# Value loads over the border of two key spans in a banded attention kernel with two expert layers

## The chip, the core and the metric

The kernel runs on one core of a Trainium2 chip. The metric is the device time of one execution in microseconds. The core has a matmul engine (TensorE, PE in the profile, with its weight loads as PEld), a vector engine (VectorE, DVE), a scalar engine (ScalarE, ACT), a general engine (GpSimd, POOL) and a sync engine (SyncE, SP), which issues nearly all loads. Each engine works its own instructions in order. Transfers run on 16 DMA engines.

## The reference

Three layers follow each other on 2 x 768 tokens of width 512. The change concerns the first, an attention in chunks of 32 queries that look at 16 keys to the left, the chunk, 8 keys to the right, and 8 memory keys:

```python
for c in range(nc):                       # chunk = 32
    c_start = c * chunk; c_end = c_start + chunk
    l_start = max(0, c_start - left_ctx)  # 16
    r_end = min(S, c_end + right_ctx)     # 8
    k_full = np.concatenate([mem_k, k[:, :, l_start:r_end]], axis=2)
    v_full = np.concatenate([mem_v, v[:, :, l_start:r_end]], axis=2)
    scores = scale * np.matmul(q[:, :, c_start:c_end], k_full.transpose(0, 1, 3, 2))
    a = np.exp(scores - np.max(scores, axis=-1, keepdims=True))
    a = a / (np.sum(a, axis=-1, keepdims=True) + 1e-09)
    out[:, :, c_start:c_end] = np.matmul(a, v_full)
```

Then comes a gated layer (`h = gelu(x @ w_in)`, halves u and v, v normalised and mixed over the tokens by `w_sg`, `x + (u * v_s) @ w_out`), and then a layer of 8 experts, in which each token takes one expert: `p[e] * (relu(x @ w1[e]) @ w2[e])`.

## The kernel before

The tokens stand in tiles of 128, 6 for each of the 2 batches (`b`, `tt`). For attention, a tile's 8 heads are two groups of four (`h4`, or `g` where loads are named), and its 128 queries two spans of 64 (`u`), each of two chunks (`c`). The host lays values out as `vw[b, tt, g, w, h, u, d]`: for each group 96 rows `w` (8 memory rows, 16 of left context, 64 own, 8 of right context), a row being 4 heads x 2 spans x 65 numbers, the 65th a one that sums the weights. Chunk 0 uses rows 0 to 63 of a span, chunk 1 rows 32 to 95 with the first 8 of them replaced by the memory rows.

The steps of a tile are `Score.load` (queries and two key tiles), `window` (POOL copies the keys of chunk 1 to `kx`), `mm` (scores, L397), `Attn.soft` (maximum on DVE, L416, exponentials on ACT, L420), `turn` (transposes, L428), and for each group of heads `Head.load` (values, L447) and `Head.s0` (32 matmuls at L463, then division by the sum at L472 to L477). `Head.load` fills one tile `v` of 128 rows for one group: partitions 0 to 63 with rows 0 to 63 and partitions 64 to 127 with rows 32 to 95, in one transfer whose source pattern has three levels:

```python
bass.AP(src.tensor, src.offset, [[32 * 8 * DV, 2], [8 * DV, 64], [1, 8 * DV]])
nc.gpsimd.tensor_copy(v[64 : 64 + NM], v[:NM])                        # L451
nc.gpsimd.tensor_scalar_mul(one, one, edge[64 * c : 64 * c + 64])     # L455
```

The copy at L451 puts the memory rows in place for chunk 1. In the first and the last tile of a batch, L455 sets the ones of rows outside the sequence to zero with the mask `edge`. Both stand on POOL directly behind the issue of the load.

`Turn` transposes the result. The classes `Conv64`, `ConvOut` and `conv_sg` turn the weights of the second layer into pairs of a high and a low part (DVE and ACT), `V`, `U`, `Gate` and `X1` are its matmuls, `route1` to `tile_experts` find the experts, and `Moe` runs the expert tiles. All loads of 128 x 512 numbers and all tiles of that size share one ring of 94 slots (`slot`); a load waits on SP for its slot.

What sets the order is the table `ORDER`: each name in it is one step of one item, issued on its engines when the table comes to it (`lv030` is the value load of batch 0, tile 3, group 0, `p030` its head's steps, `lo2` a load of output weights, `pre0` to `pre3` four early loads of the first expert's weights each, which hang on a mark that DVE writes at L1346). The engines' queues have exactly this order. `Moe.run` follows the table.

Of the kernel before, what the change touches and what calls it, by code (L numbers as in the profile page):

```python
# [12 lines left out]
F32 = mybir.dt.float32  # L13
# [6 lines left out]
ALU = mybir.AluOpType  # L20
# [33 lines left out]
a040 p021 p021 a110 lv020 p021 lq00 p020 p020 p031 k000 k001 p020 p020 p031 a041 a111 a111 p021 p031 a041 lv030
s00 p030 a11 a040 a040 a000 lv2 lv050 cv2.0 a01 cv2.0 a001 a04 t011 p030 p030 lv041 cv2.1 a001 p030 t010 a001
a000 a000 cv2.1 cv2.1 cv2.1 cv2.1 cv2.1 t010 p050 a00 a04 p041 a11 t010 cv2.2 cv2.3 lv010 p010 p010 lv040 p040
lq12 k121 t011 t011 v03.0 v03.0 p040 k120 s12 lq14 p010 p010 a121 lv100 ls3 p050 v02.0 p041 p041 p041 a120 p040
p040 v03.1 a00 lv001 a120 p001 lv051 lv000 a120 p050 p050 p051 p051 p051 p051 lq13 ls5 k130 a121 a121 t020 t020
p001 p001 p001 t020 p100 v02.0 p000 k131 v02.1 t021 t021 t021 v02.1 v02.1 s13 a131 a131 a131 p000 v04.0 v04.0
p000 lu1 cu1.0 k140 k141 p100 p100 p100 p000 s14 a140 a141 a130 a12 t000 a12 t000 v04.1 v05.0 v02.1 cu1.0 lv121  # L60
v03.1 v03.1 lv101 a140 t000 v02.1 v02.1 p101 p101 p101 lv110 p101 a140 p121 p121 p121 p110 cu1.1 lq15 k150 lv011
a130 a130 a13 a141 a141 a13 p121 lv111 p011 p011 p011 k151 s15 lo3 p011 v04.1 p111 v04.1 p111 lv130 a150 a151
p110 p110 t001 a14 t001 t001 v00.0 a150 lo0 p111 p111 p110 t100 lu2 a151 cu2.0 lu3 p130 cu2.0 consts2 a151 rx
lv131 p131 p130 p131 p131 p130 ls6 v02.1 v02.2 v05.0 v05.1 a150 a14 a15 a15 t100 t100 v05.1 v05.1 lv140 p140
v01.0 p130 p131 lv151 lx01.0 lx01.1 lv141 ls4 p141 p141 p141 p141 lv150 lu0 cu0.0 cu0.0 p150 p150 p150 cu2.1
cu2.1 lv120 p120 p120 cu2.1 t101 t101 cu2.1 p151 p120 v01.0 t101 v10.0 co0.0 p150 p140 p140 ls8 t111 t111 p120
p140 t110 t110 p151 v01.1 p151 lx00.0 p151 t121 t110 t111 cu0.1 cs3.0 cu3.0 ls0 cu3.0 cu0.1 t120 t120 cu1.1 t121
t120 v01.1 lo1 cu0.1 cu0.1 v12.0 cs8.0 v12.0 v10.0 cu0.1 cu0.1 cu0.2 cu2.1 v10.1 v10.1 cu2.1 lx00.1 lx10.0 cu1.1
lx10.1 cu1.1 cu1.1 cu2.2 v13.0 v11.0 v13.0 t121 v12.1 lx12.0 cu3.1 v01.1 cu3.1 cu3.1 cs0.0 cu3.1 ls7 cu3.1 cu3.1
v10.1 v03.1 cu1.1 cu1.2 cu0.3 v03.1 v03.1 v03.1 co0.0 cu1.3 cu3.2 v15.0 v15.0 lx11.0 v12.1 cu3.3 cu2.3 v12.1  # L70
v12.1 v11.0 v11.1 u10.0 lx11.1 v11.1 v11.1 u10.0 u10.0 v03.2 v12.1 u03.0 u03.0 u11.0 u11.0 ls2 v10.1 v10.1 v10.1
co3.0 v10.1 v14.0 v00.0 v00.1 v00.1 u10.1 v00.1 v00.1 u03.0 cs7.0 v12.1 v10.2 lx12.1 v10.2 v10.2 cs4.0 v14.0
v04.1 v04.1 v15.1 v05.1 v15.1 cs7.1 v03.2 v03.2 v14.1 u15.0 v15.1 cs5.0 u15.0 v04.1 v04.1 ls1 cs1.0 u11.0 u11.1
u01.0 v04.2 v05.1 v05.1 cs4.1 u15.0 v12.1 v12.2 v05.1 u10.1 u11.1 v00.1 v00.1 v00.1 v04.2 u10.1 v13.1 v13.1 u14.0
v00.2 u15.1 u11.1 v13.1 u01.0 v11.1 v00.2 v11.1 u14.0 u02.0 cs2.0 cs2.1 v12.2 co0.1 co0.1 u15.1 cs8.1 u01.0 u01.1
# [41 lines left out]
def tile_kernel(  # L117
# [241 lines left out]
    class Score:  # L359
# [74 lines left out]

    class Head:
# [1223 lines left out]
```

## Time and profile before

| what | value |
|---|---|
| median of 3 runs | 551.38 us (551.11 to 551.87) |
| profiled execution | 553.8 us, span 552.0 us |
| PE busy | 423.3 us (77%) |
| DVE busy | 315.7 us (57%) |
| ACT busy | 179.9 us (33%) |
| POOL busy | 77.6 us (14%) |
| bytes moved | 76.12 MB, mean 138 GB/s |

The span is the profiled execution without what lies around the program. Busy times are sums over stages that differ: the attention and the first of the weight conversions take up the first 180 us, the second layer runs to about 361 us, and the expert tiles from there to the end. The page's chain of what ended last covers only the last scatter and says nothing of the stages before; they are read from the stretches, the waits and the timelines.

### The profile page before, as it was taken

To read this page: it belongs to the slowest core of one execution; us is meant where nothing else is said; L and a number is where in the kernel's file an instruction comes from. 1 tells how busy PE (TensorE), PEld (TensorE's weight loads), DVE (VectorE), ACT (ScalarE), POOL (GpSimd) and SP (SyncE) were. 2 spreads that over 40 slices of the span, in tenths; PEclk is the share of its full clock that TensorE was granted. 3 is DMA by queue.
4 is the path that set the end of the run, shared out by engine and by line. 5 is a ranking of instruction groups with operands and counts; after the bars stand their busy time and mean duration, and the time that the engine had idled before them with its cause. 6 is when DMAs were issued, how large, how long until landed. Compare 5 with 4: busy or idle time off the path is not lost. (4 is left out here: it accounts for less than half of the span.)

```text
span 552.0 us, 10751 instructions
## 1 busy us (share of the span) xinstructions
PE 423.3 (77%) x4055; PEld 363.9 (66%) x4055; DVE 315.7 (57%) x787; ACT 179.9 (33%) x405; POOL 77.6 (14%) x154
## 2 busy tenths in 40 slices
PE   1735363836252999981998899979999999999993
PEld 0524242625141889981998797867989889696882
DVE  5725021513311799992598688948996774725450
ACT  1823020501200455430123201015765643625330
POOL 3411011211211001010000000003200302110101
PEclk9865585855675899996899899989999999999998
DMA  8631424224323000003002001379999798991000
GB/s 272 201 124 51 132 67 140 88 87 152 97 98 115 23 20 20 2 1 114 1 1 78 0 1 59 114 250 385 386 318 374 229 379 284 349 384 50 34 3 33
DMA packets 43389, 76.12 MB, mean 138 GB/s; under 512 B 5581, under 2 KB 12625, under 8 KB 43330
## 3 DMA queue, kind: packets, MB, share of 16 engines
q1 hardware_dynamic: 39362, 65.46, 35.1%
q0 software_dynamic: 2240, 6.75, 3.3%
q10 hardware_dynamic: 1728, 3.15, 1.5%
q8 instruction: 34, 0.56, 0.4%
q14 instruction: 25, 0.20, 0.1%
HBM read 69.04 MB, written 6.75 MB: 137 GB/s over the span
## 5 line engine op out<-in xcount | busy, mean ns | idle before, releaser
L463 PE MATMUL xp<-v,at 64*32 64x65 f32 x768 | 32.4, 304 | 76.3 <-DMA v<-in_vw 58.3
L188 DVE TENSOR_TENSOR we_l<-raw,we_h 128x512 fp32r<-128x512 f32 x128 | 81.3, 688 | 3.1 <-ACT we_h L183 2.3
L463 PEld LDWEIGHTS xp<-v,at 64*32 64x32 f32 x768 | 22.9, 157 | 86.7 <-issue 35.3
L183 ACT ACTIVATE we_h<-raw 128x512 fp32r<-128x512 f32 x105 | 58.7, 629 | 1.1 <-PE wot L280 1.1
L645 PE MATMUL vsp<-sg_h,vh_h 128*128 128x256 f32 x144 | 43.1, 299 | 17.0 <-DVE gtmp L658 17.0
L472 DVE TENSOR_SCALAR rs<-xp 128x4 f32<-128x4 f32 x24 | 3.6, 158 | 91.3 <-PE xp L463 91.2
L1217 PE MATMUL hp<-xe_h,we_h 128*128 128x256 f32 x160 | 45.4, 284 | 0.0
L1217 PE MATMUL hp<-xe_l,we_h 128*128 128x256 f32 x160 | 45.0, 282 | 0.0
L1217 PE MATMUL hp<-xe_h,we_l 128*128 128x256 f32 x160 | 44.9, 281 | 0.0
L645 PE MATMUL vsp<-sg_l,vh_h 128*128 128x256 f32 x144 | 42.1, 293 | 0.0
L645 PE MATMUL vsp<-sg_h,vh_l 128*128 128x256 f32 x144 | 42.0, 292 | 0.0
L1293 PE MATMUL op<-we_h,ht_h 128*128 128x512 f32 x104 | 41.8, 402 | 0.1
L1293 PE MATMUL op<-we_h,ht_l 128*128 128x512 f32 x104 | 41.1, 395 | 0.5 <-DVE ht_l L188 0.5
L1293 PE MATMUL op<-we_l,ht_h 128*128 128x512 f32 x104 | 41.1, 395 | 0.2 <-DVE we_l L188 0.2
L645 PEld LDWEIGHTS vsp<-sg_h,vh_h 128*128 128x128 f32 x144 | 29.0, 201 | 17.7 <-DVE gtmp L658 17.7
L451 POOL COPY v<-v 8x520 f32<-8x520 f32 x24 | 14.8, 616 | 127.0 <-DMA v<-in_vw 114.6
L1305 POOL DMA_INDIRECT out_dram<-o,sidx x15 | 15.8, 1054 | 119.7 <-ACT o L1304 90.8
L1217 PEld LDWEIGHTS hp<-xe_h,we_h 128*128 128x128 f32 x160 | 30.2, 189 | 0.1
L1217 PEld LDWEIGHTS hp<-xe_l,we_h 128*128 128x128 f32 x160 | 30.1, 188 | 0.0
L1217 PEld LDWEIGHTS hp<-xe_h,we_l 128*128 128x128 f32 x160 | 30.2, 189 | 0.0
L1249 DVE SCALAR_TENSOR_TENSOR ht_l<-hp,ht_h 128x512 fp32r<-128x512 f32 x20 | 13.7, 688 | 28.1 <-ACT ht_h L1248 28.1
L645 PEld LDWEIGHTS vsp<-sg_l,vh_h 128*128 128x128 f32 x144 | 29.1, 202 | 0.0
(286 smaller groups left out, 1060.4 us busy)
## 6 DMA issues: line engine op xcount, KB each, us to landing
raw<-in_w SPq DMA_DIRECT2D x160, 256.0 KB
v<-in_vw SPq DMA_DIRECT2D x24, 260.0 KB
k<-in_kw SPq DMA_DIRECT2D x24, 192.0 KB
raw_in<-in_w_in SPq DMA_DIRECT2D x16, 256.0 KB
q<-in_qT SPq DMA_DIRECT2D x12, 256.0 KB
x1d<-x ACTq DMA_DIRECT2D x12, 256.0 KB
rsg<-in_w_sgT SPq DMA_DIRECT2D x9, 256.0 KB
raw_out<-in_w_out SPq DMA_DIRECT2D x8, 256.0 KB
```

The source lines that it names most:

```text
L183: nc.scalar.activation(hi, src, AF.Copy)
L188: nc.vector.tensor_tensor(lo, src, hi.bitcast(F32), ALU.subtract)
L451: nc.gpsimd.tensor_copy(v[64 : 64 + NM], v[:NM])
L463: nc.tensor.matmul(xp[64 * u + 32 * c : 64 * u + 32 * c + 32, j, :], at[64 * c : 64 * c + 64, 2 * u + self.h4, 32 * j : 32 * j + 32], v[64 ...
L472: nc.vector.tensor_scalar_add(rs, xp[:, :, D], 1e-9)
L645: nc.tensor.matmul(self.ps[:, h * 256 : (h + 1) * 256], self.vh[s].hl[wa][:, f * 128 : (f + 1) * 128], rhs_sg(wb, s, self.g), start=(s == ...
L1217: nc.tensor.matmul(ps[:, i * 256 : (i + 1) * 256], self.w[f // 4 * 4 + k][wa][:, f % 4 * 128 : (f % 4 + 1) * 128], self.x[k // 2][wb][:, k ...
L1249: nc.vector.scalar_tensor_tensor(l, self.ps[s], 0.0, h.bitcast(F32), ALU.max, ALU.subtract)
L1293: nc.tensor.matmul(self.po[c], h[wa][:, o : o + 128], self.w[8 + k][wb], start=(k == 0 and n == 0), stop=(k == 7 and n == 2),)
L1305: nc.gpsimd.indirect_dma_start(dst, bass.IndirectOffsetOnAxis(ap=sidx[:, c : c + 1], axis=0), o, None, bounds_check=NT * 512 // n - 1, oob ...
```

## The change

A value tile no longer belongs to one group of heads. The rows of all 24 spans of keys (2 batches x 6 tiles x 2 groups, 96 rows each) are seen as one list, and load `n` takes 128 rows in a row from row 32 of span `n`: partitions 0 to 63 get rows 32 to 95 of span `n` (its chunk 1), partitions 64 to 127 rows 0 to 63 of span `n + 1` (the next one's chunk 0). There are 25 loads, `n` from -1 to 23, the first and the last of 64 rows. A head reads two tiles: chunk 0 from `vt[n - 1]`, chunk 1 from `vt[n]`. The memory rows are copied from tile `n - 1` to tile `n` in a step of its own (`mem_v`, named `m...` in the table); the masking stays with the load. The halves of the scores, of their transposes and of `edge` are swapped to match. The table `ORDER` is a new one.

```diff
 ORDER = """
-lv1 cv1.0 cv1.0 cv1.1 cv1.1 consts1 lv0 cv0.0 edges lq02 cv0.0 cv0.1 cv0.1 cv0.1 cv0.1 cv0.1 cv0.1 k021 k020 lq03
+lv0 consts1 cv0.0 edges cv0.0 lv2 cv0.1 cv0.1 cv0.1 cv0.1 cv2.0 lq01 k011 cv2.0 cv2.1 cv2.1 cv2.1 cv2.1 cv2.1
...
-                                self.sc[u][32 * j : 32 * j + 32, 2 * g + c, :],
+                                self.sc[u][32 * j : 32 * j + 32, 2 * g + 1 - c, :],
...
+    vt = {}
+
+    def load_v(n):
+        t = vt[n] = slot([128, 4, 2, DV], F32, f"v{n}")
+        p0, p1 = 64 if n < 0 else 0, 64 if n == NB - 1 else 128
+        r0 = n * W + 32
+        nc.sync.dma_start(
+            t[p0:p1].rearrange("p h u d -> p (h u d)"),
+            vw.rearrange("b t g w h u d -> (b t g w) (h u d)")[r0 + p0 : r0 + p1],
+        )
+        for p, u, m, e in ((0, 1, n, TT - 1), (64, 0, n + 1, 0)):
+            if 0 <= m < NB and m // 2 % TT == e:
+                one = t[p : p + 64, :, u, D]
+                nc.gpsimd.tensor_scalar_mul(one, one, edge[p : p + 64])
+
+    def mem_v(n):
+        nc.gpsimd.tensor_copy(vt[n][:NM], vt[n - 1][64 : 64 + NM])
...
-        def load(self):
-            b, tt, g = self.b, self.tt, self.h4
-            v = self.v = slot([128, 4, 2, DV], F32, f"v{self.n}")
-            src = vw[b, tt, g].rearrange("w h u d -> w (h u d)")
-            nc.sync.dma_start(
-                v.rearrange("p h u d -> p (h u d)"),
-                bass.AP(src.tensor, src.offset, [[32 * 8 * DV, 2], [8 * DV, 64], [1, 8 * DV]]),
-            )
-            nc.gpsimd.tensor_copy(v[64 : 64 + NM], v[:NM])
...
+                        ks = slice(64 - 64 * c, 128 - 64 * c)
                         nc.tensor.matmul(
                             xp[64 * u + 32 * c : 64 * u + 32 * c + 32, j, :],
-                            at[64 * c : 64 * c + 64, 2 * u + self.h4, 32 * j : 32 * j + 32],
-                            v[64 * c : 64 * c + 64, j, u, :], start=True, stop=True,
+                            at[ks, 2 * u + self.h4, 32 * j : 32 * j + 32],
+                            vt[n - 1 + c][ks, j, u, :], start=True, stop=True,
```

SP's queue where the value loads begin, before (`raw_in` are weights of the second layer, `q` and `k` queries and keys):

```order
L447 DMA v_573<-in_vw 128x1x520
L447 DMA v_659<-in_vw 128x1x520
L369 DMA q_663<-in_qT 128x2x256
L373 DMA k_665<-in_kw 128x384
L373 DMA k_667<-in_kw 128x384
L447 DMA v_710<-in_vw 128x1x520
L200 DMA raw_in_0_777<-in_w_in 128x512
L200 DMA raw_in_1_779<-in_w_in 128x512
L447 DMA v_781<-in_vw 128x1x520
L447 DMA v_806<-in_vw 128x1x520
```

The same place now:

```order
L445 DMA v_491<-in_vw 128x520
L445 DMA v_559<-in_vw 128x520
L445 DMA v_564<-in_vw 128x520
L445 DMA v_593<-in_vw 128x520
L371 DMA q_654<-in_qT 128x2x256
L375 DMA k_656<-in_kw 128x384
L375 DMA k_658<-in_kw 128x384
L445 DMA v_705<-in_vw 128x520
L445 DMA v-1_717<-in_vw 64x520
L445 DMA v_737<-in_vw 128x520
```

The source is 128 x 520 instead of 128 x 1 x 520, one load has 64 rows, and the loads stand in the order of the spans, so that neighbours come together.

POOL's queue at the same place, before (L177, L386: key copies; L451: memory rows; L455: mask):

```order
L451 COPY v_573<-v_573 8x520
L451 COPY v_659<-v_659 8x520
L177 COPY kx_690<-k_665 128x4x56
L177 COPY kx_690<-k_665 128x4x8
L386 COPY k_665<-k_665 64x4x16
L177 COPY kx_690<-k_667 128x4x56
L177 COPY kx_690<-k_667 128x4x8
L386 COPY k_667<-k_667 64x4x16
L451 COPY v_710<-v_710 8x520
L451 COPY v_781<-v_781 8x520
L455 TENSOR_SCALAR v_781<-v_781,edge 64x4
```

POOL's queue now (L179, L388: key copies; L455: memory rows, from the tile before; L452: mask):

```order
L455 COPY v_564<-v_559 8x520
L455 COPY v_559<-v_491 8x520
L455 COPY v_491<-v_593 8x520
L179 COPY kx_660<-k_656 128x4x56
L179 COPY kx_660<-k_656 128x4x8
L388 COPY k_656<-k_656 64x4x16
L179 COPY kx_660<-k_658 128x4x56
L179 COPY kx_660<-k_658 128x4x8
L388 COPY k_658<-k_658 64x4x16
L455 COPY v_705<-v_564 8x520
L452 TENSOR_SCALAR v-1_717<-v-1_717,edge 64x4
L452 TENSOR_SCALAR v_737<-v_737,edge 64x4
```

Each copy of memory rows names two tiles, and key copies stand between the load's mask and the next copy.

SP's queue at the last loads of the second layer's weights, before (`rsg` the mixing weights, `raw_out` the output weights, `raw` expert weights, `x1d` a row of zeros, TENSOR_LOAD an expert's number read into a register):

```order
L310 DMA rsg_2208<-in_w_sgT 128x512
L310 DMA rsg_2311<-in_w_sgT 128x512
L1126 DMA raw<-in_w 128x512 x4
L200 DMA raw_out_0_2729<-in_w_out 128x512
L200 DMA raw_out_1_2731<-in_w_out 128x512
L1126 DMA raw<-in_w 128x512 x4
L1075 DMA x1d<-zero 1x512
L1110 TENSOR_LOAD eid_97
```

The same place now:

```order
L315 DMA rsg_2189<-in_w_sgT 128x2x256
L202 DMA raw_out_0_2349<-in_w_out 128x512
L202 DMA raw_out_1_2351<-in_w_out 128x512
L315 DMA rsg_2360<-in_w_sgT 128x2x256
L312 DMA rsg_2476<-in_w_sgT 128x512
L1134 DMA raw<-in_w 128x512 x16
L1083 DMA x1d<-zero 1x512
L1118 TENSOR_LOAD eid_97
L1118 ISA x2
L1580 TENSOR_LOAD eids
```

The last output weights have moved ahead of all sixteen early expert loads, which stand in one run, and the finished table of expert numbers (`eids`) is read directly behind the first number (`eid`).

## Rows read from the trace of the kernel before

**Rows 1.** The page's 40 slices of 13.8 us: TensorE clock, transfer share, GB/s.

```profile
PEclk9865585855675899996899899989999999999998
DMA  8631424224323000003002001379999798991000
GB/s 272 201 124 51 132 67 140 88 87 152 97 98 115 23 20 20 2 1 114 1 1 78 0 1 59 114 250 385 386 318 374 229 379 284 349 384 50 34 3 33
```

**Rows 2.** Stretches: us, busy (instructions) of PE, PEld, DVE, ACT, POOL; clock, DMA share, GB/s.

```profile
0.00:180.00 180.00, 82.03 (x1657) 62.00 (x1660) 56.62 (x192) 41.03 (x136) 36.92 (x111) 0.68 0.39 125
180.00:361.00 181.00, 163.95 (x1219) 150.94 (x1209) 145.75 (x387) 52.24 (x105) 8.42 (x13) 0.94 0.10 34
361.00:552.00 191.00, 177.33 (x1192) 150.92 (x1190) 113.32 (x209) 86.64 (x164) 32.27 (x30) 0.98 0.71 248
```

**Rows 3.** Waits up to 180 us: engine, line, waited for; us, times, longest.

```profile
POOL v L451 <- DMA v<-in_vw: 114.6, 22, 8.1
...
PE xp L463 <- DMA v<-in_vw: 58.3, 15, 9.3
...
PE xp L463 <- POOL v L455: 13.1, 4, 6.5
```

**Rows 4.** Timeline of POOL, 145 to 180 us: start, us, operation [idle before].

```profile
148.04 0.61 POOL L451 COPY v<-v 8x520 f32<-8x520 f32 x1 [8.11 <-DMA v<-in_vw]
...
165.44 0.61 POOL L451 COPY v<-v 8x520 f32<-8x520 f32 x1 [4.73 <-DMA v<-in_vw]
...
178.61 0.61 POOL L451 COPY v<-v 8x520 f32<-8x520 f32 x1 [6.18 <-DMA v<-in_vw]
```

**Rows 5.** Shorter stretches, columns as in rows 2.

```profile
10.00:15.00 5.00, 2.61 (x155) 2.13 (x160) 4.03 (x11) 0.80 (x2) 4.82 (x14) 1.00 1.04 371
14.00:28.00 14.00, 9.90 (x411) 7.67 (x393) 10.52 (x33) 11.12 (x45) 6.05 (x22) 0.88 0.61 195
48.00:54.00 6.00, 4.62 (x41) 3.83 (x32) 4.53 (x12) 4.24 (x14) 0.63 (x2) 0.50 0.13 49
98.00:112.00 14.00, 10.61 (x188) 8.11 (x179) 7.41 (x22) 7.36 (x24) 2.79 (x10) 0.87 0.28 92
148.00:154.00 6.00, 2.49 (x36) 1.67 (x36) 3.39 (x9) 1.60 (x3) 1.19 (x2) 0.50 0.13 49
400.00:420.00 20.00, 20.00 (x105) 16.82 (x104) 15.50 (x27) 11.54 (x23) 0.91 (x1) 1.00 0.99 328
```

**Rows 6.** The page's DMA issues: count and KB of each.

```profile
v<-in_vw SPq DMA_DIRECT2D x24, 260.0 KB
```

**Rows 7.** Timeline, first 12 us: first load, its first reader, first matmul.

```profile
0.83 1.82 SPq L200 DMA_DIRECT2D raw_in<-in_w_in  x4
...
3.95 0.29 DVE L220 TENSOR_SCALAR cv_in<-raw_in 128x256 uint32<-128x256 uint32 x1 [3.95 <-DMA raw_in<-in_w_in]
...
11.16 0.47 PE L397 MATMUL sc<-k,q 64*32 64x64 f32 x16 [11.16 <-DMA k<-in_kw]
```

**Rows 8.** Timelines of SP, DVE and PE, 244 to 260 us.

```profile
248.76 1.75 SPq L1126 DMA_DIRECT2D raw<-in_w  x4
250.61 0.86 SPq L200 DMA_DIRECT2D raw_out<-in_w_out  x2
...
255.53 0.29 DVE L220 TENSOR_SCALAR cv_out<-raw_out 128x256 uint32<-128x256 uint32 x1 [6.84 <-DMA raw_out<-in_w_out]
...
259.56 0.58 PE L645 MATMUL vsp<-sg_h,vh_h 128*128 128x256 f32 x1 [12.75 <-DVE gtmp L658]
```

**Rows 9.** A dense stretch, columns as in rows 2.

```profile
200.00:220.00 20.00, 20.00 (x152) 19.14 (x151) 18.20 (x41) 12.78 (x25) 3.44 (x5) 1.00 0.10 27
```

**Rows 10.** Waits of SP's queue up to 180 us, columns as in rows 3.

```profile
SPq L313 <- PE xp L463: 10.4, 1, 10.4
...
SPq L369 <- POOL v L455: 4.3, 1, 4.3
```

More of the change, by code (lines that the diff above doesn't have):

```diff
@@ L29 @@
 NU = 12
+NB = 24
 UQ = 64
@@ L54 @@
[L54 to L63, printed above, removed]
@@ new lines @@
+cv1.1 k010 s01 a011 a010 a010 a011 a021 a021 cv1.1 cv1.1 cv1.1 cv1.1 k031 s03 lq05 k051 a011 cv3.0 cv1.2 a02 a031
+a031 cv0.3 a031 a010 cv3.0 cv3.1 cv3.1 k050 cv3.1 a02 lq11 k110 s05 a050 a050 k111 lq00 k001 a01 a01 k000 a030
+s11 a111 a030 a030 a111 lv020 a051 a051 a051 cv3.1 cv3.1 cv3.1 a050 a110 a110 a03 a03 s00 a000 a000 a000 lv021
+cv3.2 lv030 m030 a05 p030 a001 lv011 cv1.3 m021 p021 p030 p030 p021 p030 m020 p020 p020 p020 p020 a001 a001 a00
+a00 lq10 k100 k101 s10 a101 lv031 a110 a05 t010 m031 lv p031 lv000 p021 p021 a111 m000 a11 p031 p031 p031 p000
@@ new lines @@
+m111 p111 lu2 cu2.0 cu1.1 p120 a14 t111 v01.1 p130 p130 t110 v03.1 lu3 t110 lx01.0 lx01.1 v03.2 v03.2 p111 p111
+p111 v01.1 cs0.0 p101 p101 p101 v00.1 lo0 p140 p140 t100 p151 cu2.0 lx02.0 t111 t110 v12.0 v02.1 v00.1 cu0.0
+v02.1 v02.1 p140 lx02.1 cu2.1 cu2.1 p151 p151 p151 t101 m150 p150 t100 cu2.1 t100 cu3.0 cu3.0 t101 cu2.1 cu2.1
+v00.1 p150 p141 t101 v10.0 v02.2 p150 p150 v11.0 p140 lx11.0 p141 v04.0 cu0.1 cu2.1 cu0.1 cu0.1 p141 p141 v00.1
+v00.1 t121 v04.1 v04.1 v04.1 ls4 t120 t120 t121 v00.1 t121 t120 cu3.1 lx00.0 cu3.1 cu3.1 cu0.1 cu0.1 ls2 cu3.1
@@ new lines @@
+lg11.0 lg02.0 pre1 pre2 pre3 g14.1 g14.1 x02.1 g11.1 lg02.1 lg01.0 lg01.1 lg00.0 lg00.1 x10m0 r0 r0 r0 x12m1
+x12m2 x12m3 x12.1 x12.2 lg11.1 x02.2 x10m1 r1 x01h0 lg10.0 r1 r1 r1 r1 r1 r1 lg10.1 x10m2 x10m3 g15.1 r2 cm4
+lg12.0 lg12.1 cm5 x13m0 x13m1 R1 x10.1 R1 R1 x03h0 x05.1 r2 x01h1 x01.1 r4 x01.2 r2 r5 x13m2 r5 R2 r5 R2 R2 R2 R2
+r5 R2 x03h1 x03.1 r5 r6 r6 r6 r6 x04h0 R3 zero R3 x10.2 R2 x03.2 g15.1 r6 r6 x13m3 x13.1 x13.2 R3 RM RP r6 RP RP
+RA RA RA r5 RA RA x00h0 x00h1 x00.1 x00.2 RA RA RP RA RA x04h1 RP RP RP r5 r5 r7 x05.2 RP x04.1 r5 x11m0 x11m1
@@ L98 @@
+x11m2 x04.2 x11m3 x14m0 x11.1 x14m1 x11.2 x14m2 x14m3 x15m0 x15m1 RP RP x15m2 RA RA RP RP RP RP RP x15m3 RP RP RP
+RP R2 RP RP RP x14.1 RP RP RP RP RP RS RZ x15.1 RL XL RZ G0 cm6 cm7 r1 R4 r3 RE RT RE XL RO x15.2 RT RS x14.2 G2
+G1 RT RT RP RT XL RA XL
 """.split()
@@ L440, in __init__ @@
             self.n = f"{b}{tt}{h4}"
-        def load(self):
-            b, tt, g = self.b, self.tt, self.h4
-            v = self.v = slot([128, 4, 2, DV], F32, f"v{self.n}")
-            src = vw[b, tt, g].rearrange("w h u d -> w (h u d)")
-            nc.sync.dma_start(
-                v.rearrange("p h u d -> p (h u d)"),
-                bass.AP(src.tensor, src.offset, [[32 * 8 * DV, 2], [8 * DV, 64], [1, 8 * DV]]),
-            )
-            nc.gpsimd.tensor_copy(v[64 : 64 + NM], v[:NM])
-            for t, c in ((0, 0), (TT - 1, 1)):
-                if tt == t:
-                    one = v[64 * c : 64 * c + 64, :, c, D]
-                    nc.gpsimd.tensor_scalar_mul(one, one, edge[64 * c : 64 * c + 64])
         def s0(self):
             xp = bank([128, 4, DV], "xp")
-            at, v = attns[self.b][self.tt].at, self.v
+            at, n = attns[self.b][self.tt].at, (self.b * TT + self.tt) * 2 + self.h4
             for j in range(4):
@@ L1485, in tile_kernel @@
     at("edges", edges)
+    at("lv", load_v, -1)
     at("consts1", consts1)
@@ L1502, in tile_kernel @@
                 at(f"a{b}{i}{u}", attns[b][i].soft, u)
-                at(f"lv{b}{i}{u}", heads[b][i][u].load)
+                at(f"lv{b}{i}{u}", load_v, (b * TT + i) * 2 + u)
+                at(f"m{b}{i}{u}", mem_v, (b * TT + i) * 2 + u)
                 at(f"p{b}{i}{u}", heads[b][i][u].s0)
```

75 lines of the change are left out of this document (34 added, 41 removed).

## The prediction

> **What bounds the kernel now.** I read the page's 40 slices first. The transfer engines, which reach a busy share of 0.9 and 385 GB/s in the expert part, stand at 0.1 to 0.4 and 51 to 152 GB/s in the ten slices from 41 to 180 us, and TensorE's granted clock moves between 0.5 and 0.8 there [rows 1]. The stretches by stage say the same in sums: in the first 180 us PE is busy 82.03 us at a mean clock of 0.68, DVE 56.62, ACT 41.03, POOL 36.92, and 125 GB/s come in; from 180 to 361 us PE is busy 163.95 of 181, so that part is dense [rows 2]. No engine is the bound of the first part. The waits name what is: POOL waited 114.6 us for the value loads ahead of its copy at L451, PE 58.3 us for them directly and 13.1 us for POOL's scaling behind them [rows 3].
>
> The pace of that wait shows in POOL's timeline: from 148.04 to 178.61 us each copy comes 6.1 us after the one before (six copies, five gaps), and the last five waited 4.7 to 6.2 us for a load [rows 4]. In stretches in which only value loads are under way (48 to 54 and 148 to 154 us) 49 GB/s move at a busy share of 0.13, about 2 of 16 engines [rows 5]. That is not slow memory: per busy engine it is 49/(0.13 x 16) = 23.6 GB/s, and in the stretch from 10 to 15 us, with query, key and weight loads, 371/(1.04 x 16) = 22.3 GB/s [rows 5]. So a value load uses two engines at full rate and fourteen not at all. A load is 260 KB, 266,240 bytes [rows 6]: 266.2/49 = 5.4 us at that rate. All of SP's loads go through the same two engines, so whatever is queued behind a value load shares its pace.
>
> **The change part by part.**
>
> The loads. The source of a value load was a pattern of 2 x 64 x 520 (two overlapping windows of a span), now it is 128 x 520 without the two; the shape in the order is that of the query and weight loads, 128 rows. I take it that the load then spreads over all engines as those do: 266.2/371 = 0.72 us instead of 5.4. The bytes stay: 23 loads of 260 KB and two halves, 6,240 KB, are the 24 of before. The transfer time that leaves engines 0 and 1 is 24 x (5.4 - 0.72) = 112 us; that is the ceiling of the gain, and what is next late takes a part of it back.
>
> The Trainium skill, "DMA: Bandwidth & Descriptors", section "Why a DMA increments its semaphore by 16 and not by 1", has the count of engines as the largest number up to 16 that divides the slowest dimension of both patterns, so 2 before and 16 after. The trace agrees on the first half, by its share of 0.13 [rows 5]; no run here shows the second half yet. By that rule the sum below stands as it is; without it the third rival's 538.7 would be as near.
>
> What is next late in the first 180 us. The work there stays, so each resource's own length bounds the stage:
> - DMA: 180 us x 125 GB/s = 22.5 MB; at 371 GB/s 61 us, plus 3.1 us from the first issue to the first landing [rows 7]: 64 us.
> - ACT: 41.03 us. In its fullest stretch, 14 to 28 us, ACT is busy 11.12 of 14 (0.794) [rows 5]: 51.7 us, plus 11 us before its work begins: 63 us.
> - DVE: 56.62 at 10.52/14 = 0.751 [rows 5] is 75.4 us, plus 3.95 us until its first load lands [rows 7]: 79 us.
> - PE: 82.03 us at clock 0.68. Two attention stretches in which PE, DVE and ACT all have work have a clock of 0.88 and 0.87 and PE shares of 9.90/14 = 0.707 and 10.61/14 = 0.758 [rows 5]. Scaled by the clock, 82.03 x 0.68/0.88 = 63.4 and 82.03 x 0.68/0.87 = 64.1; divided by the shares 89.6 and 84.6; plus 11.16 us until the first matmul [rows 7]: 101 and 96 us.
> PE is the longest, so I take 97, near the denser of its two readings since the loads no longer hold either. The stage goes from 180 to 97: **83 us off**. The ends are 79 us (DVE's length, PE no obstacle) and 127 us (clock stays as it is on average: 82.03/0.707 + 11.16).
>
> The two tiles of a head. Each head's 32 matmuls now read two tiles, the halves swapped; number and form are those of before, so nothing on PE. The copy of the memory rows (24 on POOL, of 8 x 520) takes its source from the neighbouring tile: number and size stay. It is now a step of its own and no longer sits directly behind its load, so POOL's key copies don't queue behind a landing; only the eight scalings still do. What is added is that a head waits for two landings: 0 if loads run ahead, 24 x 0.72 = 17 us if each head finds the second one missing. SP issues runs of three or four value loads ahead of their copies, so I take 0 and leave 17 to the range.
>
> The order's other move. At 248.76 us SP sent four expert weight loads (they hang on DVE's mark) and only behind them the two parts of an output weight; DVE, in order, sat at that weight's conversion until 255.53, and PE 12.75 us for DVE's gate product, to 259.56 [rows 8]. The new order has all output weights ahead of all sixteen early expert loads, in one run. Nothing else was late there (both engines idle), so I take the whole **12.75 us off**; if the gap only moves, 0.
>
> From 361 us on (191.0 us [rows 2]) the sixteen loads come earlier, but SP now reads the finished table of expert numbers before its first load by number, where it had sixteen such loads ahead of that before; I set the two against each other at nothing, with 4 us either way.
>
> **Sum.** The profiled execution took 553.8 us: 553.8 - 83 - 12.75 = 458.0. The median of the runs is 2.4 us below that execution, so 455.6.
>
> **The rivals.**
> 1. Dense first stage: PE follows DVE's length, 79 instead of 97 us: 455.6 - 18 = 437.6. For it: the two engines' lengths are near each other, and 200 to 220 us shows an order that keeps both over 0.9 [rows 9]. Against: attention is a chain over POOL, PE, DVE, ACT and back for every tile, and neither of its two full stretches had PE over 0.76 [rows 5].
> 2. The clock stays low: many short matmuls with gaps leave PE at 1.2 GHz as from 48 to 54 us (0.50) [rows 5]. The stage is 127 us, the time 455.6 + 30 = 486. For it: half of that stage's slices ran so [rows 1]. Against: the gaps there are the waits for values, and 98 to 112 us had 0.87. The Trainium skill, "TensorE: Matmul & The Clock Gate", "What's actually happening", says that the throttled state is the default and activity lifts it; the trace agrees in sign, 0.50 beside 1.00 in the dense stretch from 400 us [rows 5].
> 3. The loads stay on two engines, because what confines them is the length of a row (520 numbers, as before) and not the pattern's two windows: then only the 12.75 us go: 553.8 - 12.75 - 2.4 = 538.7. Against: the weight loads' rows of 512 numbers are about as long and are among those that ran at a share of 1.04 [rows 5].
> 4. Slower: slots. All tiles come from one ring of 94 slots, a value tile now lives until two heads have read it, and SP issues in order. The first 46 loads and what is computed from them use up the ring, so the 52 loads from there to the expert weights can each have to wait for a slot. Such a wait was 4.3 us or 10.4 us where it showed [rows 10]. If all 52 paid 4.3 us unhidden, that is 224 us: 455.6 + 224 = 680. It turns the gain of 96 us into a loss from 96/52 = 1.8 us a load on. Against: the life of a slot is counted in work, and the work of the stage is done sooner.
>
> **How the numbers follow.** Forecast 62% (443 to 470), dense stage 16%, low clock 15%, two engines 3%, slots 2%; 2% that it lands within 0.2%, about what a measurement of this kernel can tell from no change. The range reaches to the first rival with the 4 us of the last part, 437.6 - 4 = 433.6, and to the second, 486, which holds the 17 us of the second tile too; what lies beyond (a third of the first two rivals, the last two and the 2%) is 17%. Faster: 62 + 16 + 15 + 3 = 96%.
>
> **What would show it.** Value loads land at over 300 GB/s, and the transfer share in the first 60 us is above 0.6; the wait of POOL and PE for values falls below 20 us in sum. The last value copy, at 178.61 us before, comes at 85 to 105 us. The gap of 12.75 us is gone. The part from the first load by expert number to the end is 187 to 195 us. Wrong if value loads keep a share of 0.13; if the attention ends before 85 or after 115 us; or if PE has a new gap of over 10 us between the attention and the routing.

## The result and the profile after

The changed kernel takes 441.75 us (median of 4 runs, 439.59 to 442.58) against 551.25 us (551.11 to 551.87): a ratio of 0.801, with an interval of 0.798 to 0.804. The profiled execution took 441.88 us, its span is 440.1 us. That is 13.9 us less than predicted, inside the range of 433.6 to 486 us and on the side that was forecast, but 1.3 us below the 443 to 470 us that had the largest chance.

The page's 40 slices of the changed kernel, 11 us each (they answer to [rows 1]; the first line is PE's busy share in tenths):

```profile
PE   0677879999999998899999689999999999999991
PEclk9898999999999999999999959999999999999996
DMA  7999890102200011000813369999789889910001
GB/s 265 364 320 364 278 315 15 49 26 73 72 25 1 1 52 45 1 1 1 300 59 130 110 214 397 331 387 363 248 269 375 283 279 396 379 41 24 19 5 40
```

The transfers that crept along for 180 us are now done in the first six slices, 66 us, at 265 to 364 GB/s a slice. The granted clock, 0.5 to 0.8 there before, is at 0.8 or more up to a single dip in front of the expert tiles.

To compare the stages I cut both kernels at two events: the end of the last matmul of the attention, and the first matmul of an expert tile (L1240 before, L1248 after). The stretches of before, cut in this way (columns as in [rows 2]: length, busy us and count of PE, PEld, DVE, ACT and POOL, granted clock, transfer share, GB/s):

```profile
0.00:182.40 182.40, 84.44 (x1697) 63.72 (x1697) 57.83 (x197) 41.94 (x138) 36.92 (x111) 0.67 0.38 123
182.40:371.80 189.40, 168.91 (x1228) 155.52 (x1225) 148.67 (x402) 51.95 (x106) 9.67 (x14) 0.94 0.14 48
371.80:552.00 180.20, 169.97 (x1134) 144.61 (x1134) 109.19 (x190) 86.03 (x163) 31.02 (x29) 0.99 0.70 248
```

And those of the changed kernel:

```profile
0.00:87.80 87.80, 63.30 (x1725) 49.65 (x1725) 63.74 (x212) 48.11 (x150) 39.45 (x113) 0.96 0.74 247
87.80:258.00 170.20, 161.13 (x1197) 147.51 (x1197) 143.53 (x388) 46.70 (x94) 10.83 (x15) 0.98 0.18 62
258.00:440.00 182.00, 171.70 (x1134) 145.95 (x1134) 109.27 (x188) 85.95 (x163) 27.83 (x27) 0.97 0.69 241
```

| part | before, us | after, us | change | of it PE's idle time | of it PE's busy time |
|---|---|---|---|---|---|
| attention | 182.4 | 87.8 | -94.6 | -73.5 | -21.1 |
| second layer and routing | 189.4 | 170.2 | -19.2 | -11.4 | -7.8 |
| expert tiles | 180.2 | 182.0 | +1.8 | +0.1 | +1.7 |

(Idle is length less busy.) Busy time falls though the matmuls are as many, 4,059 before and 4,056 after in these rows, because the clock rises from 0.67 to 0.96 in the attention. The gain of 112 us in the span is thus 85 us of waiting that is gone and 27 us that mostly the clock gave back.

What POOL, PE and DVE waited for in the first 90 us of the changed kernel (columns: engine and line, what it waited for, us in total, times, longest):

```profile
POOL kx L179 <- DMA k<-in_kw: 14.0, 8, 6.7
...
PE sc L399 <- DMA k<-in_kw: 12.3, 1, 12.3
...
DVE cv_in L222 <- DMA raw_in<-in_w_in: 4.6, 2, 4.3
...
POOL v L455 <- DMA v<-in_vw: 2.1, 4, 0.8
POOL v L452 <- DMA v<-in_vw: 1.4, 1, 1.4
```

Where POOL waited 114.6 us for values and PE 58.3 us [rows 3], POOL now waits 3.5 us and PE not at all. What is left are waits for keys and for the first weights, all while the transfer engines are full. The last copy of memory rows, at 178.61 us before [rows 4], and the last attention matmuls, from POOL's and PE's timelines (start, us, engine, line, operation):

```profile
83.84 0.61 POOL L455 COPY v<-v 8x520 f32<-8x520 f32 x1
```

```profile
86.66 1.11 PE L471 MATMUL xp<-v,at 64*32 64x65 f32 x64
```

Shorter stretches of the changed kernel (columns as above):

```profile
5.00:20.00 15.00, 4.97 (x225) 3.76 (x229) 11.47 (x34) 5.45 (x19) 5.75 (x19) 0.99 1.04 358
11.50:87.70 76.20, 63.20 (x1724) 49.56 (x1724) 58.57 (x200) 45.02 (x145) 36.50 (x97) 0.96 0.74 244
20.00:40.00 20.00, 14.79 (x505) 10.99 (x491) 15.71 (x47) 11.63 (x45) 16.07 (x43) 0.84 1.01 339
40.00:60.00 20.00, 15.95 (x487) 12.61 (x489) 11.76 (x41) 11.87 (x42) 10.14 (x32) 0.99 0.96 307
60.00:80.00 20.00, 19.79 (x386) 15.82 (x376) 17.55 (x71) 12.34 (x34) 3.92 (x7) 1.00 0.37 121
```

From 5 to 60 us the transfer engines are full; from 60 us on PE is, busy 19.79 of 20 us. So the attention has two bounds, one after the other: the bytes first, then PE.

### The profile page after: what moved, and what is told of

Same layout as the page of the kernel before. It is cut to its first block, busy times and chain, and to the rows that moved or that the text cites. A ratio compares the mean times of both kernels' runs of the same rounds, so it can differ in the third digit from the quotient of the medians.

```text
span 440.1 us, 10761 instructions
## 1 busy us (share of the span) xinstructions
PE 396.1 (90%) x4055; PEld 343.1 (78%) x4055; DVE 316.5 (72%) x787; ACT 180.8 (41%) x405; POOL 78.1 (18%) x154
## 5 line engine op out<-in xcount | busy, mean ns | idle before, releaser
L653 PE MATMUL vsp<-sg_h,vh_h 128*128 128x256 f32 x144 | 41.2, 286 | 4.2 <-DVE gtmp L666 4.0
L653 PE MATMUL vsp<-sg_l,vh_h 128*128 128x256 f32 x144 | 40.5, 281 | 0.0
L653 PE MATMUL vsp<-sg_h,vh_l 128*128 128x256 f32 x144 | 40.4, 281 | 0.0
L1313 POOL DMA_INDIRECT out_dram<-o,sidx x15 | 15.3, 1022 | 126.9 <-ACT o L1312 94.6
L653 PEld LDWEIGHTS vsp<-sg_h,vh_h 128*128 128x128 f32 x144 | 27.1, 188 | 5.0 <-DVE gtmp L666 5.0
L653 PEld LDWEIGHTS vsp<-sg_l,vh_h 128*128 128x128 f32 x144 | 27.2, 189 | 0.0
L653 PEld LDWEIGHTS vsp<-sg_h,vh_l 128*128 128x128 f32 x144 | 27.1, 188 | 0.0
L624 PE MATMUL ups<-x_h,in_l 128*128 128x256 f32 x96 | 27.0, 281 | 0.0
L624 PE MATMUL ups<-x_l,in_h 128*128 128x256 f32 x96 | 26.9, 280 | 0.0
L624 PE MATMUL ups<-x_h,in_h 128*128 128x256 f32 x96 | 26.9, 280 | 0.0
```

Of the source, the lines that this page charges most:

```text
L624: nc.tensor.matmul(ps[:, i * 256 : (i + 1) * 256], win_u[k][wa][:, f * 128 : (f + 1) * 128], xT[self.b].at(wb, k, 256 * self.g, 256), star ...
L653: nc.tensor.matmul(self.ps[:, h * 256 : (h + 1) * 256], self.vh[s].hl[wa][:, f * 128 : (f + 1) * 128], rhs_sg(wb, s, self.g), start=(s == ...
L1313: nc.gpsimd.indirect_dma_start(dst, bass.IndirectOffsetOnAxis(ap=sidx[:, c : c + 1], axis=0), o, None, bounds_check=NT * 512 // n - 1, oob ...
```

## The experiments

Theory A: a value load used two engines because its source pattern had two windows outermost; what the time does follows from the rate of the loads. Against it stand theories in which the new tiles, their sharing or the new order of issue bring the gain. Two later questions are what bounds the first stage now, and what the second term of the prediction (the gap behind `lo2`) consisted of. Medians and intervals are of four or more runs each; the kernel before took 552.3, 553.3 and 552.6 us beside the three groups of runs.

### The pattern alone: two, four and eight windows

The changed kernel, with tiles, table and matmuls as they are, but each load of 128 rows cut into 2, 4 or 8 windows outermost. So that the windows don't join into one run of rows, the host lays a spare row, which nothing reads, behind each window. For two windows:

```diff
-        r0 = n * W + 32
+        m = 8 * DV
+        a0, a1 = p0 // 64, p1 // 64
+        r0 = n * 97 + 32 + a0 * 65
...
-            vw.rearrange("b t g w h u d -> (b t g w) (h u d)")[r0 + p0 : r0 + p1],
+            bass.AP(vw.tensor, vw.offset + r0 * m, [[65 * m, a1 - a0], [m, 64], [1, m]]),
```

and correspondingly 33 rows a window for four, 17 for eight.

> The changed kernel with one thing undone: the host puts a spare row behind each span of 96, so that a value tile's source is again two windows of 64 rows with a gap between them (2 x 64 x 520), while the tiles, the two tiles of a head, the table of the order and the results stay as they are. Theory A (the number of transfer engines that a load uses is what the change is worth): the loads move at 49 GB/s again, engines 0 and 1 have 24 x 5.4 = 130 us of values and 16 MB/16 = 1 MB each of the other loads (43 us at 23 GB/s), 173 us in all where the first stage's loads now end at about 65 us; time 535 to 550 us. Theory B (the new tiles and the new order are what it is worth): 440 to 455 us.

> As k2_new_tiles, with a spare row behind every 32 rows: the source is 4 x 32 x 520. Theory A: four engines, twice the rate (about 98 GB/s alone), 65 + 43 = 108 us of transfers on the four, 43 more than now: 470 to 490 us. Theory B: 440 to 455 us.

> As k2_new_tiles, with a spare row behind every 16 rows: the source is 8 x 16 x 520. Theory A: eight engines, 32 + 43 = 75 us on the eight, 10 more than now: 445 to 455 us. Theory B: 440 to 450 us.

| windows x rows | time, us | ratio to before (interval) | last value copy at, us | POOL's wait at the copies, us |
|---|---|---|---|---|
| 2 x 64 | 529.3 | 0.956 (0.951 to 0.961) | 172.6 | 83.1 |
| 4 x 32 | 481.1 | 0.869 (0.864 to 0.874) | 122.3 | 41.9 |
| 8 x 16 | 453.0 | 0.819 (0.812 to 0.825) | 96.3 | 16.2 |
| 128 rows (the change) | 441.75 | 0.801 (0.798 to 0.804) | 83.8 | 2.1 |

The waits stand in the groups of instructions by line, of the kernels with two, four and eight windows (engine, line and operation, count, busy and mean ns of one, then the idle time before them and what ended it):

```profile
L457 POOL COPY v<-v 8x520 f32<-8x520 f32 x23 | 13.8, 611 | 83.4 <-DMA v<-in_vw 83.1
```

```profile
L457 POOL COPY v<-v 8x520 f32<-8x520 f32 x23 | 13.8, 612 | 42.2 <-DMA v<-in_vw 41.9
```

```profile
L457 POOL COPY v<-v 8x520 f32<-8x520 f32 x23 | 14.2, 634 | 22.3 <-DMA v<-in_vw 16.2 <-issue 2.6 <-PE at L430 2.6
```

The copies themselves cost the same; only the wait changes, to a half and then to less than a half. Stretches with little but value loads under way show the rate, with two windows:

```profile
84.00:88.00 4.00, 1.33 (x48) 1.08 (x48) 0.00 (x0) 0.00 (x0) 0.34 (x2) 0.50 0.13 49
88.00:92.00 4.00, 1.47 (x6) 0.90 (x6) 2.94 (x11) 0.77 (x4) 0.00 (x0) 0.50 0.13 50
```

and with four:

```profile
58.00:62.00 4.00, 1.03 (x60) 0.74 (x66) 0.00 (x0) 1.25 (x5) 2.58 (x7) 1.00 0.28 102
```

Two windows move 49 GB/s at a share of 0.13, as in [rows 5], which is 2.1 of 16 engines; four move 102 at 0.28, which is 4.5, at about the same rate per engine. The eight-window kernel has no such quiet stretch, so its rate was not isolated. What settles the number of engines for it too is the count of small packets on the pages of the kernel before, of two, four and eight windows, of the change, and of the split loads of the next section:

```profile
DMA packets 43389, 76.12 MB, mean 138 GB/s; under 512 B 5581, under 2 KB 12625, under 8 KB 43330
DMA packets 43419, 76.12 MB, mean 144 GB/s; under 512 B 5611, under 2 KB 12655, under 8 KB 43360
DMA packets 43437, 76.12 MB, mean 159 GB/s; under 512 B 5629, under 2 KB 12673, under 8 KB 43378
DMA packets 43533, 76.12 MB, mean 169 GB/s; under 512 B 5725, under 2 KB 12769, under 8 KB 43474
DMA packets 43741, 76.12 MB, mean 173 GB/s; under 512 B 5933, under 2 KB 12977, under 8 KB 43682
DMA packets 44109, 76.12 MB, mean 167 GB/s; under 512 B 6301, under 2 KB 13345, under 8 KB 44050
```

The counts under 512 B fit one small packet for each engine of each value load, if a load uses as many engines as it has windows and 16 where it is plain rows. That makes 24 x 2 = 48 before, 23 x 2 + 2 x 16 = 78, 23 x 4 + 2 x 2 = 96 and 23 x 8 + 2 x 4 = 192 for two, four and eight windows (the two half loads have one window, which is plain rows, two and four), 25 x 16 = 400 for the change and 48 x 16 = 768 for the split loads; what is left is 5,533 in all six. The Trainium skill, "DMA: Bandwidth & Descriptors", "Why a DMA increments its semaphore by 16 and not by 1", makes the number of engines the largest one up to 16 that divides the slowest dimension of both patterns; these runs agree with it, by their counts and by their shares (0.13, 0.28, and 1.01 to 1.04 with the other loads of the change).

By these rates a load takes 266.2/49 = 5.4 us, 266.2/102 = 2.6 and, as an estimate by one more doubling, 1.3; the change's is 0.72. For 23 loads the steps are 64, 30 and 13 us; the last copy moved by 50, 26 and 12.5. So about 80 to 95% of the transfer time taken from the loads reaches the end of the stage. With two windows the kernel keeps tiles, sharing and order of the change and still gains only 23 us. That is 6 to 21 us more than A had put there, a miss of A's range, while the kernels with four and eight windows lie inside theirs: the order brings some of the 23 us, and a later run shows 7 of them by a swap of two names. What is left, 88 us from two windows to all rows, is the pattern's.

### The load alone, in the old kernel

The kernel before, with each value load as two transfers of 64 rows into the same tile; tiles, matmuls and table as they were:

```diff
-            nc.sync.dma_start(
-                v.rearrange("p h u d -> p (h u d)"),
-                bass.AP(src.tensor, src.offset, [[32 * 8 * DV, 2], [8 * DV, 64], [1, 8 * DV]]),
-            )
+            for c in range(2):
+                nc.sync.dma_start(
+                    v[64 * c : 64 * c + 64].rearrange("p h u d -> p (h u d)"), src[32 * c : 32 * c + 64]
+                )
```

> The kernel before with one thing changed: each value load is two transfers of 64 x 520, one for each half of the same tile, with the old tiles, old order and old memory-row copies. Theory A: each half spreads over 16 engines, the first stage shortens to what its engines need in the old order, 88 to 100 us instead of 180: 459 to 471 us. Theory B (the order and the tiles are needed): 530 to 551 us.

457.2 us, 0.827 (0.820 to 0.834), a little below the range of A. Of the 110 us, 95 come from the loads' pattern alone. Its first stage ends earlier than that of the change; the last attention matmuls, on PE's timeline:

```profile
83.49 0.66 PE L463 MATMUL xp<-v,at 64*32 64x65 f32 x32
```

So neither the shared tiles nor the new order is needed for the attention. Two transfers of 64 rows are not quite as light as one of 128, though. SP's queue on the pages of the kernel before, of the split loads and of the change (packets, MB, share of the 16 engines' span):

```profile
q1 hardware_dynamic: 39362, 65.46, 35.1%
q1 hardware_dynamic: 40082, 65.46, 44.5%
q1 hardware_dynamic: 39714, 65.46, 43.8%
```

With the spans of 552.0, 455.8 and 440.1 us that is 194, 203 and 193 us of all engines: the same bytes keep them busy some 9 us longer. The transfers run on to 84 us at a share of 0.92, where those of the change are nearly all done at 66 us. The old stall behind the output weights stays (the waits, columns as above):

```profile
PE vsp L645 <- DVE gtmp L658: 17.6, 3, 13.3
```

### The gap behind the output weights

Two kernels swap two names in the table, so that the output weights `lo2` go out ahead of the four early expert loads `pre0`; one with the split loads, one with the old loads:

```diff
-pre0 lo2 co2.0 co2.0 co2.1 co2.1 v14.1 v13.2 g05h0 g05h0 co2.1 co2.1 g05.1 g05h1 g05h1 g05.1 u00.1 u00.1 u14.0
+lo2 pre0 co2.0 co2.0 co2.1 co2.1 v14.1 v13.2 g05h0 g05h0 co2.1 co2.1 g05.1 g05h1 g05h1 g05.1 u00.1 u00.1 u14.0
```

> split_old_tiles (457.2 us) with one pair of names swapped in the old table: lo2, the load of the third output weights, ahead of pre0, the four expert loads that hang on DVE's mark. Theory A (the 13.3 us that PE waits there for DVE's gate product are the order's other part, and they go whole): 443 to 446 us, with the changed kernel at 441.75. Theory B (the gap only moves to the next thing that is late): 452 to 457 us.

> The kernel before, its slow value loads kept, with the same swap of lo2 and pre0. Theory A: the 12.75 us of the gap go whole, 538 to 540 us. Theory B: the gap only moves, 547 to 552 us.

450.6 us (0.813, 0.807 to 0.820), 6.7 us less than without the swap, and 546.2 us (0.988, 0.982 to 0.993), 7.1 less. Both lie between what the theories had asked for: the swap is worth about 7 us, not 12.75 and not nothing. PE's gap shrinks to 5.5 us but stays (split loads and swap, PE's timeline; in brackets the idle time before and what ended it):

```profile
155.05 0.58 PE L645 MATMUL vsp<-sg_h,vh_h 128*128 128x256 f32 x1 [5.47 <-DVE gtmp L658]
```

If the rest were still a late weight, an earlier `lo2` would remove it. The next kernel, also with split loads, moves it some 120 names up:

```diff
-... u15.0 v04.1 v04.1 ls1 cs1.0 u11.0 u11.1
+... u15.0 v04.1 v04.1 lo2 ls1 cs1.0 u11.0 u11.1
...
-pre0 lo2 co2.0 co2.0 ...
+pre0 co2.0 co2.0 ...
```

> split_old_tiles with lo2 not just ahead of pre0 (450.55 us, where 5.5 us of the gap stayed because SP had a slot for that load only at 142.4 us) but some 120 names earlier in the table, ahead of ls1. Theory A (the gap is the output weight's landing alone): the remaining 5.5 us go, 444 to 447 us. Theory B (DVE is late there for a reason of its own): 449 to 452 us.

453.4 us, 0.820 (0.817 to 0.824), which does not differ from the plain swap by more than their intervals. The weight was sent at 117.88 us, 25 us sooner than by the swap, and the gap is the same (PE's timeline):

```profile
159.20 0.58 PE L645 MATMUL vsp<-sg_h,vh_h 128*128 128x256 f32 x1 [5.60 <-DVE gtmp L658]
```

The stretches around it (columns as above) show DVE full:

```profile
140.00:150.00 10.00, 10.00 (x87) 10.00 (x86) 9.83 (x21) 4.18 (x8) 0.93 (x1) 1.00 0.01 2
150.00:160.00 10.00, 4.40 (x34) 4.19 (x33) 9.00 (x23) 2.81 (x6) 0.55 (x1) 0.88 0.28 91
```

DVE is busy 9.83 and 9.00 us of 10 while PE falls to 4.40. From DVE's timeline, between the gate products `gtmp` of two tiles:

```profile
154.50 0.47 DVE L658 SCALAR_TENSOR_TENSOR gtmp<-vsp,g,b 128x256 f32<-128x256 f32 x1
...
155.62 0.29 DVE L220 TENSOR_SCALAR cv_out<-raw_out 128x256 uint32<-128x256 uint32 x1
...
158.00 0.75 DVE L238 SCALAR_TENSOR_TENSOR w_out<-raw_out,w_out 128x256 uint32<-128x256 uint32 x2
158.67 0.48 DVE L658 SCALAR_TENSOR_TENSOR gtmp<-vsp,g,b 128x256 f32<-128x256 f32 x1
```

DVE waits for nothing. It works 4.2 us without a pause between the two gate products, some 2 us of it the conversion of that weight (`cv_out`, `w_out`), all of which stands ahead of the gate product that PE needs in DVE's own queue. So of the old gap some 7 us were the late load, and 5.5 us are left to the order on DVE; no run changed that order alone, so the second part is read from the timeline and not shown by a run. In the changed kernel both are gone: PE's longest waits there are 1.9 us for a gate product and 3.4 us for gathered rows (waits from 90 to 260 us):

```profile
PE xgp L1183 <- DMA xg<-x1d,gidx: 3.4, 1, 3.4
...
PE vsp L653 <- DVE gtmp L666: 4.0, 3, 1.9
```

A last kernel of this kind takes the early expert loads `pre2` and `pre3` ahead of the routing too, as the new table does:

```diff
-lg10.0 lg10.1 lg02.1 ...
+pre2 pre3 lg10.0 lg10.1 lg02.1 ...
```

> split_lo2_early with pre2 and pre3, the last eight of the sixteen early expert loads, moved from the end of the routing to ahead of it, as in the changed kernel. Theory A (the last part is 185.4 instead of 191 us in the changed kernel because these eight no longer stand ahead of the loads by expert number): 3 to 6 us less than split_lo2_early. Theory B (they are hidden, or their slots come late): the same as split_lo2_early within 1.5 us. Either way, if 441 to 443 us is reached, what is left of the new tiles and the new table is nothing.

449.3 us, 0.811 (0.807 to 0.815), 4.1 us less, as A said. The first expert matmul comes at 264.10 us instead of 271.32, and PE's wait for the gathered rows falls from 4.5 to 1.5 us; of those 7 us the medians keep 4.1; in the profiled executions the expert tiles take 4.9 us longer (185.2 against 180.3). From here 7.5 us are missing to the changed kernel. The gap on DVE, which this kernel still has, is 5.5 of it by size; what the other 2 are, and whether tiles or table bring them, was not taken apart.

### What bounds the first stage now

Eight extra copies of 256 KB from memory to memory, which nothing waits for, in the changed kernel: once at about 14 us, where the transfer engines are full, once at about 79 us, where they are not.

```diff
+        nc.sync.dma_start(dummy[i], w1[i % NE, 0:128, 0:512])
```

> The changed kernel with eight more transfers of 256 KB (expert weights, copied within HBM to a place that nobody reads), issued by SP at about 13 us, in the stretch in which the transfer share is about 1. Theory C (with the value loads spread, the transfers bound the first 65 us): 8 x 0.72 = 5.8 us of reads, and up to twice that with the writes: 446 to 454 us. Theory D (PE and DVE bound the stage as the forecast had it): 441 to 443.5 us.

> The same eight transfers issued at about 78 us, where the transfer share is 0.07 to 0.4. Theories C and D: 441 to 443 us, the price of issuing alone.

446.2 us (0.806, 0.802 to 0.810) early, 440.4 us (0.795, 0.791 to 0.798) late. By the medians the same bytes cost 5.8 us early and nothing late; eight loads at the 0.72 us that the prediction worked out for one of 260 KB are 5.8 us, without what the writing takes. From 20 to 60 us the early copies put the share at 1.02 and 1.05 (stretches, columns as above):

```profile
20.00:40.00 20.00, 11.13 (x366) 8.12 (x348) 9.93 (x35) 9.91 (x39) 9.29 (x28) 0.67 1.02 318
40.00:60.00 20.00, 18.21 (x502) 14.53 (x503) 14.04 (x47) 11.65 (x42) 14.23 (x41) 0.91 1.05 346
```

The last value copies, early and late, on POOL's timelines:

```profile
87.50 0.61 POOL L460 COPY v<-v 8x520 f32<-8x520 f32 x1
```

```profile
84.41 0.61 POOL L460 COPY v<-v 8x520 f32<-8x520 f32 x1
```

They lie 3.1 us apart, and so do the two profiled executions (444.72 and 441.62 us). So in the first 65 us the kernel is bound by its bytes: a transfer put in front delays the end, by 3.1 us in the traces and 5.8 us by the medians for 5.8 us of reads. That it does so one for one is not shown.

PE's first matmul comes only at 12.26 us in the changed kernel. Would an earlier one help? The table with the queries and keys of two tiles ahead of the first weights:

```diff
-lv0 consts1 cv0.0 edges cv0.0 lv2 cv0.1 cv0.1 cv0.1 cv0.1 cv2.0 lq01 k011 ...
+lq02 lq01 lv0 consts1 cv0.0 edges cv0.0 lv2 cv0.1 cv0.1 cv0.1 cv0.1 cv2.0 k011 ...
```

> The changed kernel with the first two tiles' queries and keys (lq02, lq01) ahead of the first two weight loads (1 MB, 2.8 us at 371 GB/s) instead of behind them; PE's first matmul comes at 11.5 us now. Theory C (transfers bound the first 65 us, order within them is free): 440 to 443 us. Theory E (the start of PE counts): 1.5 to 3 us less, 438.5 to 440.5 us.

446.2 us, 0.808 (0.805 to 0.811), some 4 us slower, which neither theory had. PE's timeline begins so:

```profile
4.24 0.47 PE L399 MATMUL sc<-k,q 64*32 64x64 f32 x16 [4.24 <-DMA k<-in_kw]
14.14 0.47 PE L399 MATMUL sc<-kx,q 64*32 64x64 f32 x16 [9.43 <-POOL kx L179]
```

PE starts 8 us earlier and then waits 9.4 us for POOL's key copy, while DVE's first conversion moves from 4.33 to 8.67 us. PE's start was no bound; the last value copy comes at 88.24 instead of 83.84 us. The bytes are the same, so their sum alone doesn't set the end of the stage either: which load comes first counts too.

## Why the prediction was right, and where its sizes were off

The predicted 455.6 us is 13.9 us above the 441.75 measured. The first rival's 437.6 us is nearer, 4.2 us below, but not by its reason: the stage did not shrink to DVE's 79 us, and 6.5 us of the miss lie behind the attention. By the prediction's own terms:

| term | predicted | measured | share of the miss |
|---|---|---|---|
| attention | -83 | -94.6 | 11.6 |
| behind `lo2`, second layer and routing | -12.75 | -19.2 | 6.5 |
| last part | 0 (4 either way) | +1.8 | -1.8 |
| profiled execution to median | -2.4 | -0.1 | -2.3 |

**The mechanism was right.** Two engines because of two windows, the pace of 5.4 us a load, POOL and PE behind it: the runs with two, four and eight windows show the cause, and the split loads show it without any other part of the change. The third rival (the row's length confines the loads) is refuted by the changed kernel, whose rows are as long. Most of what was to show it came out: a share of 0.96 in the first 60 us (over 0.6 was named), waits for values of 3.5 us (below 20), no gap of 10 us between attention and routing. The last value copy did not: it came at 83.84 us, ahead of the 85 to 105 us that were named. The rate stood at 307 to 358 GB/s over stretches of 15 to 20 us while value loads were under way; of the page's slices two lie below the 300 that was named, 265 at the start and 278 later.

**The term of 83 us was sized by the wrong share.** The step had two factors. PE's busy time scaled by the clock, 63.4 to 64.1 us, was met by 63.20 us from 11.5 to 87.7 us, in part by luck: the clock came to 0.96 and not to 0.87 or 0.88, by which 82.03 x 0.68/0.96 = 58.1 us, and more work stands in the stage now (1,724 matmuls against 1,657). What failed is the division by PE's share, 0.707 to 0.758 from two stretches of before [rows 5]. Measured over the stage it was 63.20/76.2 = 0.83, and 0.99 from 60 to 80 us. The two stretches had been taken as full, but POOL still waited for values in them; the waits of before from 14 to 28 us, and from 98 to 112 us:

```profile
POOL v L451 <- DMA v<-in_vw: 5.3, 1, 5.3
```

```profile
POOL v L451 <- DMA v<-in_vw: 5.1, 1, 5.1
```

POOL stood still for over 5 of the 14 us in each. From 98 to 112 us this is what stopped PE; its one gap there ends, just behind the stretch, with POOL's masking of a loaded tile (PE's timeline):

```profile
112.27 1.96 PE L463 MATMUL xp<-v,at 64*32 64x65 f32 x64 [3.66 <-POOL v L455]
```

A share that is read while the suspect still holds the engine is a lower end, not the value. From 14 to 28 us it is not shown: PE lost only 0.4 us there to POOL's copy of values, and its longest gap, 2.8 us, has no cause in the profile. In the changed kernel PE's share is 0.74 and 0.80 while the bytes bind (20 to 60 us), near the two readings; the 0.99 behind that lifts the mean. The stage ends at 87.8 us, between the 97 of the forecast and the 79 of the first rival, about halfway; that is 9.2 of the term's 11.6 us, and the other 2.4 come from the cut of the stage before, at 182.4 instead of 180 us.

**The order of the bounds was missed.** I had the bytes' length, 64 us (66 measured), and took the longest resource, PE, as the bound of the whole. The runs with extra copies show that the bytes bind first, up to 65 us, and no longer at 79 us, where PE is full. The last loads still have their work behind them, some 20 us of PE with hardly a gap (busy 19.79 of 20 from 60 to 80 us), and that sum, 66 + 20 = 86 us, not the longest term, comes near the stage's 87.8. By this reading DVE's 79 us, the end of the first rival, were out of reach.

**The second term had the right place and two causes.** I gave the whole 12.75 us to the load, with both engines idle; but DVE was idle for only 6.84 of them and worked from 255.53 us on, as [rows 8] show. By the swaps 7 us were the load's, the 5.5 left stand in DVE's queue, and the new table happens to remove both. By idle time the part lost 11.4 us, near the forecast. The other 7.8 us are PE's busy time, which I had not counted: the clock is 0.98 instead of 0.94 over that part (168.91 x 0.94/0.98 = 162.0, which is 6.9 of them), and 28 matmuls more stand in the attention now, 31 fewer in this part.

**The last part** was called nothing with 4 us either way; it is +1.8 by the cut at the first expert matmul. My own sign for it, 187 to 195 us from the first load by number to the end, was missed with 185.4 us, but it measured only where that load now sits in SP's queue, at 254.67 us; the first expert matmul follows 3.4 us behind it, where it came 10.5 us behind it before (361.3 to 371.8 us).

**The offset** of 2.4 us between profiled execution and median did not carry over: the profiled execution of the changed kernel lies at its median. It belonged to one execution, not to the kernel.

**The other rivals.** The clock did not stay low: 0.96 over the stage. The Trainium skill, "TensorE: Matmul & The Clock Gate", "What's actually happening", says that activity lifts it; the rows agree in sign, 0.50 in the kernel with two windows while PE is busy a third of the time (84 to 92 us), 1.00 in the changed one while it is busy 19.79 of 20. A stretch's own share is not enough to tell the level: with four windows the clock was 1.00 from 58 to 62 us with PE busy 1.03 of 4, behind 12 us in which it was busy 10.60, and fell to 0.51 in the next 4 us. Slots cost nothing that shows: no value load waited on SP for longer than 1.4 us (the longest such wait of the first 90 us),

```profile
SPq L445 <- ACT a L422: 1.4, 1, 1.4
```

and the waits of 14.4 and 9.0 us that SP's queue had there were for mixing weights (`rsg`), for which no engine then waited longer than 0.4 us. The 24 landings that a head has to wait for more are hidden, 0 as taken.

## What to carry to other kernels

If the transfer share stands flat at a low value, 0.13 here, while an engine waits for a load, look at the outermost level of the load's pattern: two overlapping windows put 260 KB on two engines, and the time followed the number of windows (529, 481, 453 and 442 us for 2, 4, 8 and all rows). The cheap cure comes first: one transfer for each window gave 95 of the 110 us with four lines and no new layout of tiles, though it keeps the transfer engines busy some 9 us longer than one plain load would. And when one limit is lifted, a share read while it held is a lower end for what comes next; list the bounds in order of time, not only by length.

## What was not expected of the hardware

- A transfer confined to two engines is not slow on them: 49 GB/s on a share of 0.13, 102 on 0.28. With two and with four windows a busy engine moved some 23 GB/s: 49/(0.13 x 16) = 23.6 and 102/(0.28 x 16) = 22.8.
- Two transfers of 64 rows serve the attention as well as one of 128: the last copies come at 81.66 and 83.84 us. What they cost is transfer time: some 9 us more of all 16 engines for the same bytes.
- The changed kernel's first 65 us are so tightly bound that 2 MB more cost 5.8 us by the medians (3.1 us in the traces), while 65 us later they cost nothing.
- Sending the queries earlier, which started PE 8 us sooner, made the kernel 4 us slower: in a stretch bound by transfers it matters which load comes first, and here the weights that feed DVE were the better ones.
